# The signal between two heads' score products, from SyncE or from ScalarE

## Chip, cores and metric

One core of one Trainium2 chip runs the kernel. The metric is device time in microseconds (us) of one execution, as the median of several runs.

## What is computed

Attention with a threshold, and a two-layer network with a leaky ReLU on its result. There are 8 batches, 8 heads, 576 tokens and 64 dimensions a head; the network goes from 512 to 2048 and back to 512.

```
scores = (q @ k.T) / sqrt(64)
thresh = max(scores, axis=-1) - tau                 # tau = 0.02
scores = where(scores >= thresh, scores, -1e9)
attn   = exp(scores - max(scores))
attn   = attn / (sum(attn) + 1e-09)
x      = heads side by side of (attn @ v)           # 4608 x 512
h      = x @ w_in
out    = maximum(0.01 * h, h) @ w_out
```

## The kernel before, in words

The work is cut into 72 periods. A period takes four heads of one batch (two pairs, c = 0 and 1, of two heads, h = 0 and 1) and 128 query tokens. The last 64 tokens of each batch form periods of their own. Periods are numbered by `st.n`, and the Python loop over `n` at the end of the kernel writes out, engine by engine, what stands in each. Nothing reorders it afterwards: each engine runs its list in the order of the program, and waits are semaphores between the lists.

In period n, PE (TensorE) does in this order: the scores of period n (L297, 24 matmuls: queries and keys are split into a high and a low 16-bit half and multiplied in three combinations, `i` = 0, 1, 2); transposes of the queries or keys of later periods (L186); a transpose that spreads the reciprocal sums (L410); a piece of the network's second layer (L479); a piece of its first layer (L466); the product of weights and values of period n - 2 (L426); and again a piece of the second and of the first layer.

VectorE copies the scores out of PSUM with the row minimum of their negatives (L338), makes the thresholds (L356) and masks three of the four score tiles (L378). ScalarE has, per period: a plain exponential for each of these three tiles (L367); two leaky ReLUs of the first layer (L469); copies of transposed queries, keys and sums (L249 or L246, L416); every other period the evacuation of the second layer's bank (L488); and for the fourth tile the steep pass: a Prelu with slope 1e20 (L372) and an exponential that sums (L373), both written by `exp_steep`. This tile needs no mask from VectorE. In steady periods ScalarE's order is L249, L416, L367, L488 (every other period), L469, L367 twice, L469, L372, L373.

SP (SyncE) issues in each period a DMA transpose of the previous period's weights (L389, `turn_w`), which waits for L373 and for VectorE's masks; then loads of later queries, keys and values (L75, L99) and stores of finished rows (L496, L502). A DMA's issue occupies its queue, so what stands behind it waits.

The two heads of a pair use the upper and the lower 64 rows of PE's array and run side by side. All scores of a period lie in one PSUM tile of five banks. The bank of columns 1024 to 1535 is shared: `b12`, a piece of head 1, lies in it, and so does `a12`, a piece of head 0. [...] `scores` therefore puts b12 first among head 1's products and a12 last among head 0's, and orders a signal between them: an instruction without work (`nop`, L331) on another engine waits for the last matmul of b12, and the first weight load of a12 waits for the `nop`. The list `SIGNAL` says which engine gives it: GpSimd in periods 0, 1 and 3 to 8, SP in period 2 and from period 9 on (63 signals). On SP the `nop` of period n stands behind the loads and stores of period n - 1 and ahead of the transpose of the weights of period n - 1.

Of the kernel before, what the change touches and what calls it, by code (L numbers as in the profile page):

```python
# [33 lines left out]
def kernel(  # L34
# [10 lines left out]
    nc = tc.nc  # L45
# [182 lines left out]
    def take_high(keys, parts=1):  # L228
        for key in keys:
            for i in range(2 if key[2] == "t" else parts):  # L230
                dst, tp = place32(key, 0, i, parts)
                nc.scalar.activation(out=dst, in_=tp, func=AF.Copy, bias=0.0, scale=64.0)
# [41 lines left out]
    def pieces(c, h):  # L274
        a = PLACE[c, h]
        cut = (a // 512 + 1) * 512
        return [(a, cut - a), (cut, a + 576 - cut)]

    SIGNAL = [nc.gpsimd, nc.gpsimd, nc.sync] + [nc.gpsimd] * 6 + [nc.sync]
    HALVES = ((0, 0), (1, 0), (0, 1))  # L280

    BEHIND = mybir.DependencyInfo(mybir.DependencyClass.Sync, mybir.DependencyReason.DATA)
# [1 line left out]
    def product(st, c, h, piece, i):  # L284
        a, n = piece
        qx, kx = HALVES[i]
        rows = ds(64 * h, 64)
        key0 = 64 * (1 - h) + a - PLACE[c, h]
        for u in range(2 if st.tail else 1):
            pair = 2 * c + u if st.tail else 2 * st.pp + c  # L290
            if st.tail:
                lhs = turned[st.b, "q"][rows, qx, pair, MAIN:S]
                o = sc[ds(64 * u, 64), ds(a, n)]
            else:
                lhs = turned[st.b, "q"][rows, qx, pair, ts(st.m, 128)]
                o = sc[:, ds(a, n)]
            yield nc.tensor.matmul(out=o, lhsT=lhs, rhs=turned[st.b, "k"][rows, kx, pair, ds(key0, n)],  # L297
                                   start=(i == 0), stop=(i == 2), skip_group_check=True)
# [3 lines left out]
    def scores(st, between=None):  # L302

        st.mn = sb.tile([128, 4], FP32, tag="mn", bufs=2, name="mn")
        st.th = sb.tile([128, 4], FP32, tag="th", bufs=2, name="th")
        st.s, st.e = {}, {}
        (a00, a01), (b01, b00) = pieces(0, 0), pieces(0, 1)
        (a11, a12), (b12, b11) = pieces(1, 0), pieces(1, 1)
        todo = [[(0, a00), (0, a01), (1, a11), (1, a12)], [(1, b12), (1, b11), (0, b01), (0, b00)]]
        if st.n < 2:  # L310

            todo[1] = todo[1][2:] + todo[1][:2]
        todo = [[(c, x, i) for c, x in row for i in range(3)] for row in todo]
        at_, signal, first = [0, 0], None, None
        while todo[0] or todo[1]:
            if between and todo[0][0][0] == 1 and todo[1][0][0] == 1:
                between()
                between = None
            h = 1 if not todo[0] or (todo[1] and at_[1] < at_[0]) else 0
            if between and todo[h][0][0] == 1:  # L320
                h = 1 - h
            c, x, i = todo[h].pop(0)
            at_[h] += x[1]
            for mm in product(st, c, h, x, i):
                if first is not None:
                    tc.declare_no_dep(mm.ins, first.ins, reason="other banks")
                if (h, x) == (0, a12) and i == 0:
                    tc.add_manual_dep(mm.ins, signal.ins.name, BEHIND, reason="the row halves share a bank")
                last = mm
            if (h, x) == (1, b12) and i == 2:  # L330
                signal = SIGNAL[min(st.n, 9)].nop()  # L331
                tc.add_manual_dep(signal.ins, last.ins.name, BEHIND, reason="the row halves share a bank")
            if (h, x) == (0, a11) and i == 2 and st.n:
                first = copy_min(st, 0)

    def copy_min(st, n):
        st.s[TILES[n]] = sb.tile([128, 576], FP32, tag=f"s{n}", bufs=1, name="s")
        return nc.vector.tensor_scalar(  # L338
            out=st.s[TILES[n]][:, :], in0=sc[:, ds(PLACE[TILES[n]], 576)], scalar1=-1.0 / UNIT, scalar2=None,
            op0=AX.mult, op1=AX.min, accum_out=st.mn[:, n : n + 1])  # L340
# [19 lines left out]
    def w_of(st, t):  # L360
        c, h = t
        return st.w[:, c, :, :].rearrange("q n d -> q (n d)")[:, ds(576 * h, 576)]

    def exp_plain(st, n):
        t = TILES[n]
        st.e[t] = sb.tile([128, 576], FP16, tag=f"e{n}", bufs=1, name="e")
        nc.scalar.activation(out=st.e[t][:, :], in_=st.s[t][:, :], func=AF.Exp, bias=st.mn[:, n : n + 1], scale=-1.0)  # L367

    def exp_steep(st, n):
        c, h = t = TILES[n]  # L370
        z = st.s[t][:, :]
        nc.scalar.activation(out=z, in_=z, func=AF.Prelu, bias=st.th[:, n : n + 1], scale=-1.0, alpha=1e20)  # L372
        nc.scalar.activation(out=w_of(st, t), in_=z, func=AF.Exp, bias=minus_tau[:, :], scale=1.0,  # L373
                             accum_out=st.sum[:, c, h : h + 1])
# [77 lines left out]
    def settle():  # L452
        l2q.extend(pending)
        pending.clear()
# [18 lines left out]
    def layer2():  # L473
        g, r = l2q.pop(0)
        if r == 0:
            g.o = ps.tile([128, 512], FP32, tag="o", bufs=1, name="o")
        for j in (2 * r, 2 * r + 1):
            for c in range(2):
                nc.tensor.matmul(out=g.o[ds(64 * c, 64), :], lhsT=g.g[:, j, ds(64 * c, 64)],  # L479
                                 rhs=w_out16[:, j, :], start=(j == 0), stop=(j == 15), skip_group_check=True)  # L480
        if r == 7:
            g.out = sb.tile([128, 512], FP32, tag="osb", bufs=3, name="osb")
            if g.where == (B - 1, 3):
                a = nc.scalar.activation(out=g.out[0:64, :], in_=g.o[0:64, :], func=AF.Copy, bias=0.0, scale=1.0)
                x = nc.vector.tensor_copy(out=g.out[64:128, :], in_=g.o[64:128, :])
                tc.declare_no_dep(x.ins, a.ins, reason="other rows")
            else:
                nc.scalar.activation(out=g.out[:, :], in_=g.o[:, :], func=AF.Copy, bias=0.0, scale=1.0)  # L488
            stores.append(g)
# [141 lines left out]
    N = len(periods)  # L631
    n = 0
    while n < N + PV_LAG or l1q or pending or l2q or stores:
        st = periods[n] if n < N else None
# [8 lines left out]
        if n == 0:  # L643
            def between():
                copy_min(st, 0)
                copy_min(st, 1)
                take_low(k32[1])
                for x in now32:
                    turn32(x)
            scores(st, between)  # L650
            turn32(late)
        elif st:
            scores(st)
# [67 lines left out]
        for half in range(2):  # L721
            if half == 1 and n in (3, 4):
                exp_steep(st, plain)
            for _ in range(2):
                if l2q:
                    layer2()
            if l1q:
                layer1()
            elif n >= N:
                settle()  # L730
            if half == 0:
                if st:
                    for i in range(1, plain if n else 0):
                        exp_plain(st, i)
                        if n == 3 and i == 1:
                            take_high(late)
                if here:
                    take_w(before, 6, 6, o[:, 0:768], on_act)
                if late and n not in (0, 3):
                    turn32(late)  # L740
                    take_high(late)
                if n == N:

                    before.wt = sb.tile([128, 2, 9, 128], FP16, tag="wT", bufs=4, name="wT")
                    free = [(sc[:, ts(i, 512)].bitcast(FP16), 8 * i, m) for i, m in enumerate((8, 8, 2))]
                    for o, first, m in free:
                        turn_w_here(before, first, m, o)
                if due and n <= N:
                    if n != 3:
                        pv(due)  # L750
                    evacuate(due)
                if n == N:
                    a, *more = [take_w(before, first, m, o[:, 0 : 128 * m], on_dve if first else on_act)
                                for o, first, m in free]
                    for x in more:
                        tc.declare_no_dep(x.ins, a.ins, reason="other banks")
            elif st and n != 3:
                for i in range(plain + (n == 4), 4):
                    exp_steep(st, i)
        if n == 4:  # L760
            take_low(late)
        for i in range(plain if st else 0):
# [37 lines left out]
```

## Time and profile before

| | |
|---|---|
| median of 3 runs | 483.92 us (483.92, 486.24, 481.17) |
| the profiled execution | 484.03 us |
| its span, first to last instruction | 482.3 us |
| granted TensorE clock in it | 1.000 |
| PE busy | 463.1 us (96%) |
| VectorE (DVE) busy | 433.2 us (90%) |
| ScalarE (ACT) busy | 420.1 us (87%) |
| GpSimd (POOL) busy | 216.2 us (45%) |
| DMA transposes of weights (L389) | 68, median 6.1 us from issue to landing |

In a line of the timeline stand the start and the time that the group spans, both in us, the engine, the line of the kernel, the operation, what it writes and reads, its shape, how many there are, and in brackets how long the engine was idle before and what released it. SPq and ACTq are the instruction queues of these engines; an event semaphore there is a wait, a signal or both. PEld is PE's weight load. In a list of waits the numbers are the total in us, how often, and the longest.

### The profile page before, as it was taken

The numbers are of one execution on the slowest core, as the hardware profiler recorded it, in microseconds if no ns is written. First come the engines' busy times: TensorE is split into PE (matmuls) and PEld (weight loads), VectorE is DVE, ScalarE is ACT, GpSimd is POOL, SyncE is SP. The second block draws the span as 40 slices with busy tenths as digits, with TensorE's granted clock in tenths as the row PEclk, the third lists the DMA queues.
The fourth block names the chain that finished last, engine by engine and source line by source line (L and its number), as shares of the span: only waits on it lengthen the run. The fifth ranks groups of instructions, "written<-read, shape, count | busy, mean of one in ns | idle before, by whom it ended". The sixth has DMA issues, their size and how long they took to land.

```text
span 482.3 us, 25139 instructions
## 1 busy us (share of the span) xinstructions
PE 463.1 (96%) x10810; PEld 375.7 (78%) x10810; DVE 433.2 (90%) x1309; ACT 420.1 (87%) x783; POOL 216.2 (45%) x355
## 2 busy tenths in 40 slices
PE   6889889999999999999999999999999999999996
PEld 4668667888888888888888888788888778877774
DVE  3999879999999999999999999999999989999940
ACT  4899779999999999999999999899999889988862
POOL 2645547554565464454465474454466563000000
PEclk9999999999999999999999999999999999999999
DMA  9999999798999978899799988889889995655641
GB/s 176 237 217 197 164 206 201 160 196 182 205 171 202 209 161 188 155 173 211 154 190 202 212 174 201 135 183 193 185 183 193 200 165 124 124 122 123 127 91 46
DMA packets 206271, 83.67 MB, mean 173 GB/s; under 512 B 175280, under 2 KB 200880, under 8 KB 206160
## 3 DMA queue, kind: packets, MB, share of 16 engines
q1 hardware_dynamic: 199184, 74.66, 80.1%
q0 software_dynamic: 5568, 6.95, 7.8%
q8 instruction: 84, 1.38, 1.2%
q10 hardware_dynamic: 1408, 0.46, 0.4%
q14 instruction: 27, 0.22, 0.1%
HBM read 36.70 MB, written 9.44 MB: 96 GB/s over the span
## 4 chain that ended last, share of the span: by engine, by line
PE 86%; DMA 5%; DVE 4%; ACT 2%; issue 1%; SPq 1%; DVEq 0%; ACTq 0%
PE hp L466 25%; PE o L479 25%; PE sc L297 21%; PE pv L426 8%; DMA wT<-w 4%; PE tp L410 3%; PE tp L186 3%; DVE s L338 2%; DVE w L378 1%; DMA raw<-in_k_dram 1%; ACT g L469 1%; DVE qT L239 0%; SPq L86 0%; ACT e L367 0%; DVE kT L239 0%
## 5 line engine op out<-in xcount | busy, mean ns | idle before, releaser
L338 DVE TENSOR_SCALAR_CACHE_REDUCE s<-sc 128x576 f32<-128x576 f32 x288 | 205.5, 753 | 17.4 <-PE sc L297 17.4
L466 PEld LDWEIGHTS <-win 128*64 128x64 f16 x4608 | 146.5, 110 | 28.7 <-DVE xt L437 1.1
L378 DVE SCALAR_TENSOR_TENSOR w<-s,th,e 128x576 f16<-128x576 f32 x213 | 163.8, 817 | 0.2
L367 ACT ACTIVATE e<-s,mn 128x576 f16<-128x576 f32 x213 | 157.8, 778 | 0.0
L479 PE MATMUL o<-wout,g 128*64 128x512 f16 x1152 | 148.8, 379 | 0.3 <-DMA wout<-in_moe_w_out_dram 0.3
L466 PE MATMUL hp<-x,win 128*64 128x128 f16 x4096 | 136.3, 219 | 0.6 <-DVE x L445 0.3
L469 ACT ACTIVATE g<-hp 128x512 f16<-128x512 f32 x144 | 86.1, 598 | 43.7 <-PE hp L466 43.7
L297 PE MATMUL sc<-kT,qT 64*128 64x384 f16 (+7 forms) x1920 | 120.7, 284 | 3.5 <-DVE s L338 1.3
L297 PEld LDWEIGHTS <-qT 64*128 64x128 f16 (+1 forms) x1920 | 90.1, 97 | 20.3 <-issue 2.0
L160 POOL TENSOR_SCALAR scaled<-raw 128x512 f32<-128x512 f32 x53 | 32.7, 616 | 144.8 <-DVE w L378 131.8
L479 PEld LDWEIGHTS <-g 128*64 128x64 f16 x1152 | 58.7, 110 | 29.1 <-issue 0.4
L171 POOL TENSOR_TENSOR half<-scaled,half 128x512 f16<-128x512 f32 (+1 forms) x68 | 71.6, 1054 | 5.8
L373 ACT ACTIVATE w<-s,minus_tau 128x576 f16<-128x576 f32 x75 | 58.2, 776 | 2.4
L372 ACT ACTIVATE s<-s,th 128x576 f32<-128x576 f32 x75 | 57.5, 767 | 0.7 <-DVE th L356 0.7
L426 PE MATMUL pv<-wT,v 128*64 128x128 f16 (+1 forms) x1600 | 53.1, 215 | 5.2 <-DMA wT<-w 3.7
L426 PEld LDWEIGHTS <-v 128*64 128x64 f16 x1600 | 45.8, 110 | 6.9 <-issue 3.7
L167 POOL CAST half<-scaled 128x512 f16<-128x512 f32 (+1 forms) x68 | 38.3, 563 | 4.4
L445 DVE TENSOR_TENSOR x<-pv,by 128x256 f16<-128x256 f32 x64 | 27.1, 424 | 8.1 <-PE pv L426 7.0
L416 ACT COPY by<-tp 128x256 f16<-128x256 f16 x72 | 26.8, 372 | 0.0
L186 PEld LDWEIGHTS <-half 64*128 64x128 f16 x968 | 24.2, 95 | 2.5 <-issue 1.0
L113 POOL CAST v<-vraw 128x256 f16<-128x256 f32 x64 | 24.5, 417 | 0.0
L186 PE MATMUL tp<-ident,half 64*128 64x64 f16 x968 | 24.1, 190 | 0.0
(61 smaller groups left out, 332.9 us busy)
## 6 DMA issues: line engine op xcount, KB each, us to landing
vraw<-in_v_dram SPq DMA_DIRECT2D x16, 512.0 KB, 5.4
out_dram<-osb SPq DMA_DIRECT2D x31, 256.0 KB, 3.9
raw<-in_q_dram SPq DMA_DIRECT2D x13, 512.0 KB, 4.9
raw<-in_k_dram SPq DMA_DIRECT2D x13, 512.0 KB, 5.6
win<-in_moe_w_in_dram POOLq DMA_DIRECT2D x4, 512.0 KB, 10.7
wout<-in_moe_w_out_dram POOLq DMA_DIRECT2D x4, 512.0 KB, 12.5
raw<-in_q_dram SPq DMA_DIRECT2D x12, 128.0 KB, 3.8
raw<-in_k_dram SPq DMA_DIRECT2D x10, 128.0 KB, 4.3
```

The lines of the kernel that those rows point to most:

```text
L171: nc.gpsimd.tensor_tensor(out=halves[key][:, 1, 0:n, :, :], in0=scaled.pop(key)[:, 0:n, :, :], in1=halves[key][:, 0, 0:n, :, :], op=AX.sub ...
L186: nc.tensor.transpose(tps[key][r][:, x, t, :], half[rows, x, t, :, :].rearrange("p h d -> p (h d)"), ident[rows, rows])
L297: yield nc.tensor.matmul(out=o, lhsT=lhs, rhs=turned[st.b, "k"][rows, kx, pair, ds(key0, n)], start=(i == 0), stop=(i == 2), skip_group_ch ...
L338: return nc.vector.tensor_scalar(out=st.s[TILES[n]][:, :], in0=sc[:, ds(PLACE[TILES[n]], 576)], scalar1=-1.0 / UNIT, scalar2=None, op0=AX. ...
L367: nc.scalar.activation(out=st.e[t][:, :], in_=st.s[t][:, :], func=AF.Exp, bias=st.mn[:, n : n + 1], scale=-1.0)
L372: nc.scalar.activation(out=z, in_=z, func=AF.Prelu, bias=st.th[:, n : n + 1], scale=-1.0, alpha=1e20)
L373: nc.scalar.activation(out=w_of(st, t), in_=z, func=AF.Exp, bias=minus_tau[:, :], scale=1.0, accum_out=st.sum[:, c, h : h + 1])
L378: st.last = nc.vector.scalar_tensor_tensor(out=w_of(st, t), in0=st.s[t][:, :], scalar=st.th[:, n : n + 1], in1=st.e[t][:, :], op0=AX.is_le ...
L426: nc.tensor.matmul(out=st.pv[ds(64 * h, 64), c, ts(u, n)], lhsT=v16[st.b % 2][:, pair, blk, :], rhs=st.wt[:, c, blk - (blk > 4), ts(u, n)] ...
L466: nc.tensor.matmul(out=hp[ds(64 * c, 64), jj, :], lhsT=w_in16[:, i, ds(128 * (4 * u + jj) + 64 * c, 64)], rhs=g.x[:, i, :], start=(i == 0) ...
L469: nc.scalar.activation(out=g.g[:, ds(4 * u, 4), :], in_=hp[:, :, :], func=AF.Prelu, bias=0.0, scale=1.0, alpha=0.01)
L479: nc.tensor.matmul(out=g.o[ds(64 * c, 64), :], lhsT=g.g[:, j, ds(64 * c, 64)], rhs=w_out16[:, j, :], start=(j == 0), stop=(j == 15), skip_ ...
```

## The change

From period 9 on, ScalarE gives the signal. The steep pass of a period's fourth tile is no longer written out at the end of its own period but kept in a list, `behind_signal`, and written out in the next period's `scores`, right behind the signal. So ScalarE's queue has the signal of period n + 1 between the second L469 of period n and the steep pass (L372, L373) of period n. The earlier periods and the last one keep their order. Lines of the kernel behind the edits have numbers that are higher by 1, 3 or 7.

```diff
-    SIGNAL = [nc.gpsimd, nc.gpsimd, nc.sync] + [nc.gpsimd] * 6 + [nc.sync]
+    behind_signal = []
+    SIGNAL = [nc.gpsimd, nc.gpsimd, nc.sync] + [nc.gpsimd] * 6 + [nc.scalar]
...
             if (h, x) == (1, b12) and i == 2:
                 signal = SIGNAL[min(st.n, 9)].nop()
                 tc.add_manual_dep(signal.ins, last.ins.name, BEHIND, reason="the row halves share a bank")
+                while behind_signal:
+                    behind_signal.pop(0)()
...
             elif st and n != 3:
                 for i in range(plain + (n == 4), 4):
-                    exp_steep(st, i)
+                    if 9 <= n + 1 < N:
+
+                        behind_signal.append(lambda st=st, i=i: exp_steep(st, i))
+                    else:
+                        exp_steep(st, i)
```

In the built program PE's, VectorE's and GpSimd's lists are the same as before but for the semaphore that PE's 63 weight loads wait for. ScalarE's list has 63 event semaphores more, SP's has 63 fewer.

## The prediction

> **What bounds the kernel now.** I read the page's busy times first, then the chain that ended last, then PE's timeline of one steady period, then the waits by engine, and last the timelines of SP and ScalarE beside PE's. Busy time and chain agree that PE sets the end:
>
> ```profile
> PE 463.1 (96%) x10810; PEld 375.7 (78%) x10810; DVE 433.2 (90%) x1309; ACT 420.1 (87%) x783; POOL 216.2 (45%) x355
> PE 86%; DMA 5%; DVE 4%; ACT 2%; issue 1%; SPq 1%; DVEq 0%; ACTq 0%
> ```
>
> So a change counts only by how much it moves PE. One steady period on PE:
>
> ```profile
> 251.58 1.64 PE L297 MATMUL sc<-kT,qT 64*128 64x384 f16 x24
> 253.06 0.40 PE L186 MATMUL tp<-ident,half 64*128 64x64 f16 x16
> 253.39 0.30 PE L410 MATMUL tp<-ident,rec 128*64 128x128 f16 x4
> 253.52 1.03 PE L479 MATMUL o<-wout,g 128*64 128x512 f16 x8
> 254.39 1.06 PE L466 MATMUL hp<-x,win 128*64 128x128 f16 x32
> 255.28 0.73 PE L426 MATMUL pv<-wT,v 128*64 128x128 f16 x20
> 255.84 1.03 PE L479 MATMUL o<-wout,g 128*64 128x512 f16 x8
> ```
>
> The next scores start at 257.69, so a period is 6.11 us and its 24 score products run without a gap. Here the signal is not on the path. In the trace its event on SP stands at 252.116, 0.54 us after the scores start; the weight load that needs it starts at 252.579, 0.08 us behind the load before it, which is PE's pace. A signal reaches a waiting load in 0.04 us (the smallest distance seen), so 0.4 us is spare.
>
> The waits from 360 to 400 us, and then PE and SP there, show where it is late:
>
> ```profile
> PEld L297 <- SPq L331: 1.8, 2, 1.1
> PE sc L297 <- SPq L331: 1.1, 2, 0.8
> ```
>
> ```profile
> 382.64 0.50 PE L297 MATMUL sc<-kT,qT 64*128 64x256 f16 x5 [0.34 <-SPq L331]
> ...
> 387.61 1.32 PE L297 MATMUL sc<-kT,qT 64*128 64x384 f16 x19
> 389.74 0.50 PE L297 MATMUL sc<-kT,qT 64*128 64x256 f16 x5 [0.81 <-SPq L331]
> ```
>
> ```profile
> 383.28 5.25 SPq L389 DMA_TRANSPOSE wT<-w  x1
> 388.58 1.04 SPq L502 DMA_DIRECT2D out_dram<-osb  x2
> ```
>
> SP issued a transpose for 5.25 us and then two stores, so its signal, next in the queue, came at 389.67 where 388.15 would have been in step. The products that it stands for, the first three of the second head, had ended at 388.11. Of the 63 signals from period 9 on, three made PE wait: at 277.08, 382.64 and 389.73.
>
> ScalarE around the place where the signal is to go:
>
> ```profile
> 251.69 0.60 ACT L469 ACTIVATE g<-hp 128x512 f16<-128x512 f32 x1 [0.39 <-PE hp L466]
> 252.18 0.77 ACT L372 ACTIVATE s<-s,th 128x576 f32<-128x576 f32 x1
> 252.98 0.77 ACT L373 ACTIVATE w<-s,minus_tau 128x576 f16<-128x576 f32 x1
> ...
> 253.76 0.56 ACT L249 COPY kT<-tp 128x512 f16<-128x512 f16 x1
> 254.22 0.37 ACT L416 COPY by<-tp 128x256 f16<-128x256 f16 x1
> 254.48 0.78 ACT L367 ACTIVATE e<-s,mn 128x576 f16<-128x576 f32 x1
> 255.16 0.59 ACT L488 ACTIVATE osb<-o 128x512 f32<-128x512 f32 x1
> ```
>
> ScalarE waits for PE ahead of L469, then runs without a pause to L488, the evacuation of the output bank, which PE needs for its second layer at 255.84.
>
> **Removed: 63 signals on SP.** The gain is what PE lost to late ones. Score starts 380.98, 387.61 and 394.70 make periods of 6.63 and 7.09 us against 6.11: 0.52 + 0.98 = 1.50 us. The late one at 277.08 costs nothing: its period is 6.13. In all other periods the cover is SP being early. SP also saves an event and its successor's 0.08 us in each period, worth nothing: the transpose behind it waits for the steep pass of L373 anyway and starts 0.12 us after it ends in 67 of 68 cases. Loads and stores stay in their order. Bounds for the gain: 0 if PE then waits elsewhere for the same queue, and about 3 us if this execution is a mild one (the three runs span 481.17 to 486.24).
>
> Would PE wait elsewhere? The transpose of 383.28 landed at 390.51, and PE needs it for the pv product at 392.29, which would come at 392.29 - 0.66 - 1.12 = 390.51 (the two late loads, 0.74 and 1.20 us behind their neighbours, less 0.08 each). That is just in time. I keep 1.50.
>
> **Added: 63 signals on ScalarE, each with a wait for PE.** Queued behind it are L372, L373, then the copies, L367 and L488; SP's transpose waits for L373, PE for the copies, DVE for e, PE for L488. First the signal: L469 itself waits for the layer product just ahead of the scores and starts 0.11 us after they do, so the event can go at the same 0.54 us at which SP's goes now, in every period, with 0.4 us to spare. No PE time is lost on it.
>
> Now the delay of L372. Today its own event, which checks VectorE, stands at 251.697, 0.006 us after L469 starts, and L372 starts at 252.184, 0.10 us before L469 ends. In the new order the signal goes 0.427 us after the start of L469; the next event follows a signal by 0.078 us on SP's and GpSimd's queues; on ScalarE an instruction starts 0.056 us after its event when the engine is free (L249 at 191.99). That gives 0.561 us against 0.493 today: a delay of 0.07 us. The trace has no signal on ScalarE, so I bound it: 0.00 if event and dispatch hide in L469's run, and 0.24 if the signal goes only when L469 has ended (0.597 + 0.078 + 0.056 - 0.493). I take 0.07, because both rows it is built from are of this mechanism.
>
> [...] The trace shows an overlap of 0.10.
>
> Who feels 0.07 us? For each PE instruction that waits for ScalarE I took its start less the end of the releaser. Layer one after L469 has 0.46 us or more in nine of ten cases, pv after L416 0.62, VectorE's masks after e 0.37; these cover it. The output bank after L488 has not: 0.05 us is the handing over itself, and most of the 33 cases after 80 us stand at 0.05 to 0.09. Taking 0.068 less the spare of each (and less ScalarE's pauses ahead of L488) leaves 17 cases and 0.58 us. At 0.24 it would be 4.5 us, at 0.00 nothing. In the periods without L488 ScalarE's 0.22 us pause ahead of L469 takes it up.
>
> SP's transposes start 0.07 us later too. Five periods are already 0.12 to 0.21 us long because pv waits for a landing (pv at 175.00 is one); 5 x 0.07 = 0.34 us. At 0.24 it is 1.2.
>
> **The steep pass that is recorded later** now stands behind VectorE's masks and ahead of the next period's copies in the program's text. Each engine's own list is the same but for the signals: PE, VectorE and GpSimd unchanged, ScalarE +63 events, SP -63. Cost nothing; the only waits with other numbers are PE's on the signal.
>
> **Sum.** The profiled execution took 484.03 us (span 482.3): 484.03 - 1.50 + 0.58 + 0.34 = 483.45. It stands 0.11 above the median of 483.92. Predicted: 483.4 us, within 1% of before, which is about what a measurement of this kernel can tell from no change.
>
> **Rivals.**
> *Slower: the signal waits for L469's end.* Place: ScalarE, each period. Price: delay 0.24, so 4.5 us at the output bank and 1.2 at landings, less 1.50: 484.03 + 4.2 = 488.2. It decides once the delay passes 0.11 us, where banks (1.2) and landings (0.5) eat the gain. Against it: the event of L372 goes 0.006 us after L469 starts, not after its end. [...]
> *Faster: late signals are what makes the runs differ.* If the median of runs loses 3 us of them, 484.03 - 3.0 + 0.9 = 481.9. For it: 5 us between three runs, and SP's transposes take 2.5 to 7.2 us to issue. Against it: only three of 63 signals were late here, in an execution at the median.
> *Nothing gained: the transfer is the wait.* PE reaches pv earlier and stands there for the transpose: 484.03 + 0.9 = 484.9. For it: the zero margin at 390.51.
> *The signal comes no earlier.* Only if ScalarE itself were late; its pause ahead of L469 is 0.22 us or more in every period from 10 on. Practically out.
>
> **How the numbers follow.** Forecast 0.50; landing wait 0.20; late signals 0.17; L469's end 0.13. The forecast alone spans 482.5 to 484.2, its delay going from 0.00 to 0.10 us (at 0.10: banks 1.13, landings 0.50). The range goes to 481.0 on the side of the late signals and to 486.4 on the other, about half way to 488.2. Faster than 479.1 takes more late signals than any run here shows room for: 0.04. Slower than 488.8 takes the delay of 0.24 with no gain: 0.06. Within: 0.90.
>
> **What would show it.** Right: no wait of L297 for a signal; the two periods near 385 back at 6.1 us; L372 starting 0.56 us after L469 rather than 0.49; PE's second-layer start after L488 at 0.05 us throughout. Wrong: L372 at 0.7 us or more; pv waiting for wT by as much as the signal did; or periods that are longer everywhere by over 0.1 us.

## The result and the profile after

| | before | after |
|---|---|---|
| median of 22 runs each, us | 482.34 | 484.33 |
| lowest and highest, us | 480.18 and 486.24 | 481.39 and 488.42 |
| the profiled execution, us (its span) | 484.03 (482.3) | 484.98 (483.2) |
| granted TensorE clock in it | 1.000 | 0.996 |

The ratio is 1.0044, with a 95% interval of [1.0023, 1.0064]: slower by about 2 us. One run of the change, at 490.26 us, is left out of its highest time and of the ratio because it lies over 1.5% above the fastest. The time lies within 1% of before and within the predicted range, but on the other side of no change than the forecast. The first three runs of before had a median of 483.92 us, and the forecast's sum started from one of 484.03; over 22 runs the median is 482.34.

Lines behind the edits have higher numbers now: L466 and L469 (layer one and its leaky ReLU) are L469 and L472, L372 and L373 (the steep pass) are L375 and L376, L479 and L488 (layer two and its evacuation) are L482 and L491, L426 (pv) is L429, L331 (the signal) is L332.

Busy times and shares of the chain of the changed kernel:

```profile
PE 465.6 (96%) x10810; PEld 379.3 (78%) x10810; DVE 432.6 (90%) x1309; ACT 424.6 (88%) x783; POOL 216.1 (45%) x355
PE 83%; DMA 6%; ACT 5%; DVE 4%; issue 2%; SPq 0%; DVEq 0%
```

PE bounds it as before. ScalarE's share of the chain went from 2% to 5%, and that of SP's queue from 1% to 0. Its waits from 72 to 415 us (total, how often, longest):

```profile
ACT s L375 <- ACT g L472: 1.5, 6, 0.3
...
PE pv L429 <- DMA wT<-w: 0.6, 2, 0.3
PE o L482 <- ACT osb L491: 0.5, 3, 0.2
```

No wait for the signal is in that list: the lines `PEld L297 <- SPq L331` are gone, and nothing like them has come on ScalarE's queue. The three rows shown are among those that before's list doesn't have. ScalarE and PE in the steady period that the prediction showed:

```profile
253.06 0.60 ACT L472 ACTIVATE g<-hp 128x512 f16<-128x512 f32 x1 [0.39 <-PE hp L469]
253.63 0.78 ACT L375 ACTIVATE s<-s,th 128x576 f32<-128x576 f32 x1
254.44 0.78 ACT L376 ACTIVATE w<-s,minus_tau 128x576 f16<-128x576 f32 x1
...
255.94 0.78 ACT L370 ACTIVATE e<-s,mn 128x576 f16<-128x576 f32 x1
256.62 0.59 ACT L491 ACTIVATE osb<-o 128x512 f32<-128x512 f32 x1
```

```profile
252.94 1.65 PE L298 MATMUL sc<-kT,qT 64*128 64x384 f16 x24
256.64 0.72 PE L429 MATMUL pv<-wT,v 128*64 128x128 f16 x20
257.26 1.05 PE L482 MATMUL o<-wout,g 128*64 128x512 f16 x8
258.12 1.09 PE L469 MATMUL hp<-x,win 128*64 128x128 f16 x32
259.14 1.07 PE L298 MATMUL sc<-kT,qT 64*128 64x384 f16 x15
```

In before, the groups behind the second layer's start at 255.84 were:

```profile
256.70 1.06 PE L466 MATMUL hp<-x,win 128*64 128x128 f16 x32
257.69 1.65 PE L297 MATMUL sc<-kT,qT 64*128 64x384 f16 x24
```

L375 starts 0.57 us after L472 where it was 0.49. The delay runs on through ScalarE to L491, whose end PE awaits: L482 starts 0.62 us after pv where it was 0.56, it and the group behind it take 1.05 and 1.09 where they took 1.03 and 1.06, and the period is 6.20 where it was 6.11.

ScalarE at 104 us, and PE's second layer behind it, show what the forecast had not at all:

```profile
104.36 0.60 ACT L472 ACTIVATE g<-hp 128x512 f16<-128x512 f32 x1 [0.47 <-PE hp L469]
105.21 0.77 ACT L375 ACTIVATE s<-s,th 128x576 f32<-128x576 f32 x1 [0.26 <-ACT g L472]
```

```profile
108.84 1.05 PE L482 MATMUL o<-wout,g 128*64 128x512 f16 x8 [0.17 <-ACT osb L491]
```

Here ScalarE stood idle for 0.26 us with all waits met: the last event ahead of L375 ends at 104.885, L375 starts at 105.210. It happens in periods 14, 23, 32, 41, 50 and 59, the six cases of the list above. I call it a pause. In 14, 32 and 50 an evacuation of the bank follows, and these three periods take 6.47 us.

Where the two late signals had been, PE now stands a little later, for the transposed weights:

```profile
393.32 0.75 PE L429 MATMUL pv<-wT,v 128*64 128x128 f16 x20 [0.28 <-DMA wT<-w]
```

**Where the time went.** From the start of period 10 to that of period 64 before took 334.2, 334.2 and 334.4 us in its three profiled executions, the change 334.9 and 336.6 in its two. For each of these periods I took its length less the shortest that it has in any run of this study whose order of work is like the change's or before's. That excess falls into three parts. "Banks" are all excesses below 0.1 us, "pauses" periods 14, 32 and 50 above that, the rest is irregular (late signals, landings). In us:

| | banks | pauses | irregular | sum |
|---|---|---|---|---|
| before, three profiled executions | 0.26, 0.33, 0.44 | 0 | 2.67, 2.57, 2.69 | 2.99 in the mean |
| the change, two | 1.47, 1.40 | 1.08, 1.08 | 1.17, 2.92 | 4.56 in the mean |

Banks and pauses cost 2.2 us more (the three paused periods hold 3 x 0.084 of bank wait, too). The irregular part is smaller by 0.6 here, and by 0.86 over all nine executions of this study with the signal on ScalarE at its normal place (1.79 against 2.64 in the mean). The net of these parts, 1.3 to 1.6 us, compares with 1.7 to 2.1 us by the ratios of the repeated runs (1.0036 in e9 and 1.0044 here); the rest is within what single executions scatter.

### The profile page after: what moved, and what is told of

Its sections match the earlier page's. It is cut to its first block, busy times and chain, and to the rows that moved or that the text cites. A ratio compares the mean times of both kernels' runs of the same rounds, so it can differ in the third digit from the quotient of the medians.

```text
span 483.2 us, 25140 instructions
## 1 busy us (share of the span) xinstructions
PE 465.6 (96%) x10810; PEld 379.3 (78%) x10810; DVE 432.6 (90%) x1309; ACT 424.6 (88%) x783; POOL 216.1 (45%) x355
## 4 chain that ended last, share of the span: by engine, by line
PE 83%; DMA 6%; ACT 5%; DVE 4%; issue 2%; SPq 0%; DVEq 0%
PE hp L469 24%; PE o L482 24%; PE sc L298 20%; PE pv L429 8%; DMA wT<-w 5%; PE tp L413 3%; PE tp L186 3%; DVE s L341 2%; ACT g L472 1%; DMA raw<-in_k_dram 1%; ACT s L375 1%; DVE w L381 1%; ACT w L376 1%; ACT e L370 1%; ACT kT L249 1%
## 5 line engine op out<-in xcount | busy, mean ns | idle before, releaser
L469 PEld LDWEIGHTS <-win 128*64 128x64 f16 x4608 | 147.9, 110 | 28.4 <-issue 1.3
L482 PE MATMUL o<-wout,g 128*64 128x512 f16 x1152 | 149.5, 380 | 0.5 <-ACT osb L491 0.5
L469 PE MATMUL hp<-x,win 128*64 128x128 f16 x4096 | 137.4, 220 | 0.6 <-DVE x L448 0.3
L472 ACT ACTIVATE g<-hp 128x512 f16<-128x512 f32 x144 | 86.1, 598 | 39.4 <-PE hp L469 37.2
L482 PEld LDWEIGHTS <-g 128*64 128x64 f16 x1152 | 60.4, 110 | 29.2 <-issue 1.2
L376 ACT ACTIVATE w<-s,minus_tau 128x576 f16<-128x576 f32 x75 | 58.2, 776 | 2.4
L375 ACT ACTIVATE s<-s,th 128x576 f32<-128x576 f32 x75 | 58.2, 776 | 2.4 <-ACT g L472 1.5
L429 PE MATMUL pv<-wT,v 128*64 128x128 f16 (+1 forms) x1600 | 53.1, 215 | 4.5 <-DMA wT<-w 3.0
L429 PEld LDWEIGHTS <-v 128*64 128x64 f16 x1600 | 45.8, 110 | 5.7 <-DMA wT<-w 2.7
```

The source lines that it names most:

```text
L429: nc.tensor.matmul(out=st.pv[ds(64 * h, 64), c, ts(u, n)], lhsT=v16[st.b % 2][:, pair, blk, :], rhs=st.wt[:, c, blk - (blk > 4), ts(u, n)] ...
L469: nc.tensor.matmul(out=hp[ds(64 * c, 64), jj, :], lhsT=w_in16[:, i, ds(128 * (4 * u + jj) + 64 * c, 64)], rhs=g.x[:, i, :], start=(i == 0) ...
L472: nc.scalar.activation(out=g.g[:, ds(4 * u, 4), :], in_=hp[:, :, :], func=AF.Prelu, bias=0.0, scale=1.0, alpha=0.01)
```

## The experiments

Two theories were put to the test. A: the loss is made on ScalarE, because an instruction that waits for PE stands in its queue, and it is felt at the output bank. B: it comes from SP, whose transposes now start elsewhere, and from their landings. Within A two readings of the pauses stood open: A1, they are bound to a count of ScalarE's instructions (they come 128 apart if events and reads of the accumulator are counted); A2, they are bound to the place behind the signal.

**e1_between: the signal between the two halves of the steep pass.** The Prelu is written out at once, only the summing exponential stands behind the signal.

```diff
-    def exp_steep(st, n):
+    def exp_steep(st, n, later=False):
...
+        if later:
+            behind_signal.append(lambda: exp_sum(st, n))
+        else:
+            exp_sum(st, n)
...
-                        behind_signal.append(lambda st=st, i=i: exp_steep(st, i))
+                    exp_steep(st, i, later=9 <= n + 1 < N)
```

> The signal stays on ScalarE, but stands between the two halves of the steep pass: the Prelu ahead of it, the summing exponential behind. Theory A (the signal holds ScalarE's queue, so the Prelu starts late and the output bank is evacuated late): the Prelu starts 0.49 us after the leaky ReLU as before, not 0.57; the 0.84 us starts are gone; second-layer waits for the output bank fall back to the handing over; no wait of PE for a signal; ratio to before 0.997 to 1.001. Theory B (the time comes from SP: with its signals gone, transposes and loads go at other moments, and PE waits for landings): this changes nothing on SP against the changed kernel, so ratio 1.003 to 1.006.

Measured 481.66 us, ratio to before 0.9982 [0.9953, 1.0011]. Its ScalarE and PE:

```profile
251.01 0.60 ACT L480 ACTIVATE g<-hp 128x512 f16<-128x512 f32 x1 [0.39 <-PE hp L477]
251.51 0.77 ACT L375 ACTIVATE s<-s,th 128x576 f32<-128x576 f32 x1
252.31 0.78 ACT L384 ACTIVATE w<-s,minus_tau 128x576 f16<-128x576 f32 x1
...
254.49 0.59 ACT L499 ACTIVATE osb<-o 128x512 f32<-128x512 f32 x1
```

```profile
255.16 1.03 PE L490 MATMUL o<-wout,g 128*64 128x512 f16 x8
256.02 1.06 PE L477 MATMUL hp<-x,win 128*64 128x128 f16 x32
257.02 1.64 PE L298 MATMUL sc<-kT,qT 64*128 64x384 f16 x24
```

The Prelu is back at 0.49 us, layer two at 1.03, the period at 6.11, no pause can be seen, and no signal is late: the event goes at 251.442, behind the Prelu in the queue. The engine that signals is the same as in the change, and SP's list too, so the place in ScalarE's queue makes the loss. Where it is felt, e1 alone leaves open: SP's transposes, too, start again 2.29 us after the scores as in before (median), where they start at 2.38 in the change. e3 tells the two apart.

**e2_phase: four tiny activations more at the start,** so that every later instruction of ScalarE has a number higher by four.

```diff
-    nc.scalar.activation(out=waste[:, :], in_=minus_tau[:, :], func=AF.Exp, bias=0.0, scale=1.0)
+    for _ in range(5):
+        nc.scalar.activation(out=waste[:, :], in_=minus_tau[:, :], func=AF.Exp, bias=0.0, scale=1.0)
```

> The changed kernel with four tiny activations more at the start, where ScalarE waits for the first loads; they shift the place in ScalarE's instruction count by 4. Theory A1 (a pause of 0.27 us at every 128th instruction of ScalarE, which the changed kernel's 128 instructions per nine periods pin to the Prelu behind the signal): the six Prelu starts at 0.85 us after the leaky ReLU are gone, all at 0.57 to 0.60; the three periods of 6.47 us are 6.20; ratio 1.002 to 1.003. Theory A2 (the pause belongs to what these periods do): the six stay where they are, ratio 1.004.

Measured 484.47 us, ratio 1.0048 [1.0028, 1.0068]. The six starts at 0.85 us are gone and periods 14, 32 and 50 take 6.20: A1 holds, A2 doesn't. A ratio of 1.002 to 1.003 had been expected; the time did not fall. Its profile has one long wait for a landing that the change's has not:

```profile
PE pv L429 <- DMA wT<-w: 1.5, 1, 1.5
```

**e3_bank_first: the evacuation of the output bank ahead of the first plain exponential,** everything else as in the change.

```diff
-            exp_plain(st, 0)
+            if n < 9:
+                exp_plain(st, 0)
...
+            if half == 0 and st and n >= 9:
+                exp_plain(st, 0)
```

> The changed kernel, but from period 9 on ScalarE evacuates the output bank ahead of the first plain exponential of the period. Theory A: the 0.08 us at the Prelu and the 0.27 us pauses stay, but PE's second-layer start no longer waits (spare of 0.5 us or more in place of 0.05); steady periods at 6.11; ratio 0.998 to 1.001. Theory B: the bank was not the place, ratio 1.003 to 1.006. If VectorE's masks now wait for the exponential, periods grow, ratio over 1.004.

Measured 482.81 us, ratio 1.0009 [0.9979, 1.0039]. ScalarE and PE near the end of the evacuation:

```profile
252.43 0.60 ACT L491 ACTIVATE osb<-o 128x512 f32<-128x512 f32 x1
252.93 0.77 ACT L370 ACTIVATE e<-s,mn 128x576 f16<-128x576 f32 x1
...
255.64 0.60 ACT L472 ACTIVATE g<-hp 128x512 f16<-128x512 f32 x1
256.21 0.78 ACT L375 ACTIVATE s<-s,th 128x576 f32<-128x576 f32 x1
```

```profile
253.68 1.03 PE L482 MATMUL o<-wout,g 128*64 128x512 f16 x8
254.54 1.06 PE L469 MATMUL hp<-x,win 128*64 128x128 f16 x32
```

The Prelu is as late as in the change (0.57) and pauses six times, but L491 ends 0.65 us before PE needs it (median; below 0.06 in none of 33 cases), and layer two takes 1.03 again. The bank excess falls to 0.17 us, and the steady periods with a bank take 6.11 again. SP's transposes start as late as in the change (2.38 us after the scores). So the output bank is where the delay is felt, and B is out as the main cause. The trace carries this, not the time, whose interval overlaps that of the change.

**e4_later: the signal waits for two products more,** to see what a larger delay costs.

```diff
-            if (h, x) == (1, b12) and i == 2:
+            if (h, x, i) == ((1, b11, 0) if st.n >= 9 else (1, b12, 2)):
```

> The changed kernel, but its signal waits for the first product of the next piece of the same head, two products later. Theory A: the Prelu starts some 0.15 us later again (0.70 to 0.75 us after the leaky ReLU); about 17 to 22 output-bank waits grow by that, 2.5 to 3.5 us in all; ratio 1.008 to 1.012. The signal itself still has 0.2 us to spare. Theory B: no change against the changed kernel, ratio 1.003 to 1.006.

Measured 488.73 us, ratio 1.0133 [1.009, 1.0175].

```profile
254.19 0.60 ACT L472 ACTIVATE g<-hp 128x512 f16<-128x512 f32 x1 [0.39 <-PE hp L469]
254.92 0.78 ACT L375 ACTIVATE s<-s,th 128x576 f32<-128x576 f32 x1
```

The Prelu starts at 0.74 us (median), 26 of 33 banks make PE wait, and the steady ones of their periods take 6.36: 0.25 for a delay of 0.25. It cost more than forecast, 6 us, and one for one with the delay in these periods.

**e5_both: e1 and e3 together.**

> Both remedies at once: the signal between Prelu and summing exponential, and the output bank evacuated ahead of the first plain exponential. Theory A: no wait for a signal, none for the bank; steady periods all 6.11 us, so also the 0.04 us that five bank waits cost before are gone; ratio to before 0.995 to 1.000. If the landings of the transposes are what is left, PE's waits for wT stay and vary from run to run by 1 to 2 us.

Measured 481.56 us, ratio 0.9988 [0.996, 1.0016]. No bank makes PE wait (0.65 us spare), but two periods are long for landings (6.64 and 7.19). Against e1 nothing is gained that can be measured.

**e6_behind: only the engine of the signal changes;** the steep pass stays at the end of its period and so ahead of the signal.

```diff
-    SIGNAL = [nc.gpsimd, nc.gpsimd, nc.sync] + [nc.gpsimd] * 6 + [nc.sync]
+    SIGNAL = [nc.gpsimd, nc.gpsimd, nc.sync] + [nc.gpsimd] * 6 + [nc.scalar]
```

> ScalarE gives the signal, but its steep pass stands ahead of it in the queue, so only the order of the two is undone. If a signal goes as soon as the instruction ahead has left ScalarE's wait (the exponential waits for the Prelu's end, 1.29 us after the leaky ReLU starts), it comes 1.4 us after the scores start where 0.96 is needed: PE waits 0.45 us in each of 63 periods, 28 us in all, ratio 1.05 to 1.07. If it goes only when the instruction ahead has ended, 0.8 us more: 75 to 85 us, ratio 1.15 to 1.18. If ScalarE's place in the queue did not matter: ratio 1.00.

Measured 499.58 us in two runs, ratio 1.0347 [1.0286, 1.0408]. Its waits and ScalarE (line numbers as before):

```profile
PEld L297 <- ACTq L331: 24.0, 52, 0.5
...
PE sc L297 <- ACTq L331: 7.3, 46, 0.2
```

```profile
252.81 0.77 ACT L372 ACTIVATE s<-s,th 128x576 f32<-128x576 f32 x1
253.60 0.78 ACT L373 ACTIVATE w<-s,minus_tau 128x576 f16<-128x576 f32 x1
```

The signal goes at 253.611, 0.007 us after L373 starts and 0.77 before it ends: here the event did not wait for the end of what stood ahead of it. The order in the queue is worth 17 us. Less was lost than expected, since a late weight load cost PE 0.14 us less than it waited: 0.48 us of wait made each period 0.33 longer (6.45 against 6.11).

**e7_before_again and e8_before_again: the kernel before, profiled twice more.**

> The kernel before, profiled once more, to see whether late signals belong to it. If the 1.5 us of PE waits for the signal are a part of this kernel, two or three of its 63 signals on SP are late again, near 277, 383 and 390 us. If they were chance of the one execution, they are absent or elsewhere, and the gain that the change could have is smaller than 1.5 us.

> As the run ahead of it: a third look at the kernel before, for how many signals on SP are late and what they cost in sum; 1.5 us again if they are a part of the kernel, 0 to 1 us if they are chance.

Measured 482.96 and 483.84 us, one run each. The late signals recur, with 1.22 and 2.35 us of load waits in the two. The second's, from 72 to 415 us:

```profile
PEld L297 <- SPq L331: 2.3, 3, 1.2
PE sc L297 <- SPq L331: 1.3, 2, 0.9
```

Their periods are longer by 0.69 and 1.87 us, by 1.50 in the first execution: 1.35 in the mean. They are a part of the kernel and no accident of one run.

**e9_change_again and e10_between_again: the change and e1 on the same chip.**

> The changed kernel once more, beside the next run on the same chip: ratio to before 1.002 to 1.006. In its profile the six late Prelu starts of 0.85 us stand at the same instructions and 16 to 18 output-bank waits are there; both come from ScalarE's order alone and do not vary. PE's waits for landings do vary and stand where the late signals of before stood, near periods 42 and 60, if SP's queue and the transfers are what these signals were late for.

> The signal between Prelu and summing exponential, once more. Theory A gives 2.2 us less than the changed kernel on the same chip (1.4 of bank waits, 0.8 of pauses): ratio to before 0.996 to 1.001, and 0.994 to 0.997 against the changed kernel. Whether it beats before depends on how much of the late signals' time comes back as waits for landings: all of it and the ratio is 1.000, none and it is 0.996.

The change 484.31 us, 1.0036 [1.0014, 1.0058], with the same six pauses and the same banks. Its waits for landings were expected near periods 42 and 60; the long ones came in 43 and 57. e1's kernel 482.38 us, 0.9978 [0.9953, 1.0003], so 1.9 us below the change by the medians. It beats the change; against before its two intervals both still touch 1. From period 10 to 64 its two executions took 332.5 and 333.2 us, below all three of before.

**e11_phase_again and e12_phase_one: four tiny activations at the start once more, and one.** The diff is e2's, with `range(2)` in e12.

> The changed kernel with four more tiny activations on ScalarE at the start, a second time, because the first profile showed the six pauses gone from the Prelu and yet the time was not lower. If the pauses are part of the loss: the Prelu starts at 0.57 us after L472 in periods 14 to 59, periods 14, 32 and 50 take 6.20 us, and the ratio to before is 1.0020 to 1.0030, about 0.8 us below the changed kernel's 1.0036 to 1.0044. If what the pauses cost is given back at landings of the transposed weights, or is not felt: the profile is the same but the ratio stays at 1.0036 to 1.0048.

> The changed kernel with one more tiny activation on ScalarE at the start, so that each 128th instruction is the second L472 of a period rather than the Prelu behind the signal. L472 is preceded by 0.2 to 0.4 us in which ScalarE waits for TensorE. If the pause is bound to the count of instructions: no Prelu of periods 14 to 59 at 0.85 us after L472, and L472 starts at the usual distance behind the layer product or up to 0.27 us later in six periods. If the pauses are part of the loss, the ratio to before is 1.0020 to 1.0030; if they are not felt, or given back at landings, 1.0036 to 1.0048.

e11 482.75 us, 1.0012 [0.999, 1.0034]; e12 483.94 us, 1.0038 [1.0007, 1.0068]. In e11 the pauses are gone again. In e12 they are not, against what I expected:

```profile
104.61 0.60 ACT L472 ACTIVATE g<-hp 128x512 f16<-128x512 f32 x1 [0.47 <-PE hp L469]
105.48 0.78 ACT L375 ACTIVATE s<-s,th 128x576 f32<-128x576 f32 x1 [0.27 <-ACT g L472]
```

But they have moved by exactly one instruction. In the change the time passes between the last event ahead of L375 (104.868) and L375 (105.210), 0.34 us for 0.06 elsewhere. In e12 it passes between the signal (105.042) and that event (105.415), 0.37 us for 0.08, and L375 follows the event by 0.06. I had left the events out when I reckoned that one step leads to L472; the number counts them. So A1 is shown to the instruction. What the pauses cost in the repeated runs isn't: on one chip the kernel without them was 1.2 us faster at the median (in the mean 1.6, interval about [0.1, 3.1]), but e2, the same kernel as e11, had shown nothing. Its 1.0048 and e11's 1.0012 also say that a ratio repeats less well than one interval tells.

## Why the prediction was right and wrong

**The step that failed: "added", what the delay costs.** The prediction set 0.58 us at the output bank and 0.34 at landings against a gain of 1.50, and so forecast 0.6 us less. The runs show 1.3 to 1.4 us at the bank and a further 0.8 that no term held, against a gain of about 0.9. That the forecast of 483.4 stands only 0.9 us from the measured 484.33 is partly luck: its starting point was 1.7 us above the median of before.

**Right: the signal is never late on ScalarE.** It goes 0.54 to 0.57 us after the scores start in all of periods 10 to 63 (predicted 0.54), the weight load follows it by 0.44 us or more without waiting, and the two periods near 385 lost their waits for it.

**Right: the rival of L469's end is out.** e6 shows the event 0.007 us behind the start of the instruction ahead of it, and 0.77 us before that one's end.

**Right but small: the delay.** Predicted 0.07 us, measured 0.084 (0.493 to 0.577); event to event is 0.080 where 0.078 was taken, event to start 0.062 for 0.056. L375 now starts 0.02 us before L472 ends, where the overlap had been 0.10.

**In the step "added", the place was right and the size wrong.** The output bank feels the delay (e3), but the term of 0.58 us measures 1.3 to 1.4 (banks 1.44 - 0.34, and 3 x 0.084 in the paused periods). The spare of the 33 cases was known to a few hundredths, and the term hangs on them: 0.016 us more of delay adds that in each of some 17 cases, and a wait of 0.06 us cost PE 0.084, since layer one behind it also took 0.02 longer to the next scores (1.02 us from start to start, in e1 1.00).

**What no step held: ScalarE's pause,** 0.27 to 0.29 us, six times, 128 instructions apart, three of them ahead of a bank: 3 x 0.27 = 0.8 us. In before the event of L372 stood 0.006 us after L469's start, and 0.487 us before L372's, so the queue was half a microsecond ahead of the engine. e6, with the order of before, shows that such a lead hid the pause: in the same six periods the event of L373, which has the numbers 192 to 832 in the order of the queue, follows that of L372 by 0.37 to 0.38 us instead of 0.087, and the Prelu starts at 0.494 us all the same. The signal, which waits for PE, takes this lead away: in the change 0.062 us lie between the event and the start of L375. Nine periods hold 119 instructions of ScalarE in before and 128 in the change, so in the change the pause comes back to the same instruction every nine periods, and it is the one behind the signal.

**The step "removed": the 1.50 us.** The amount is there in three executions (1.35 in the mean), but only about 0.9 comes back, a figure good to some 0.5, since landings scatter. The prediction saw the zero margin of the transpose at 390.51 and kept the 1.50 all the same. In the changed kernel PE waits for a landing there (0.28 us at 393.32, behind the latest of the signals, and 0.30 at 281.58). That was the rival "the transfer is the wait", and by these means it holds for about a third of the sum.

**Landings, 0.34,** can't be told from the scatter of landings between executions (irregular 0.88 to 2.92 us with the signal on ScalarE).

So the sum with the measured terms is 484.03 - 0.9 + 1.4 + 0.8 = 485.3 against 484.98 of the profiled execution. That they come so close is in part chance: from period 10 to 64 these two executions differ by only 0.7 us, because few landings were late in the change's; another 0.4 arose ahead of period 10, and 0.2 was saved behind 64.

The rival "late signals make the runs differ" fell: they are gone, and the runs still spread by 7.0 us. The traces show a larger source: period 10 starts between 76.1 and 80.0 us in the 14 profiled executions, while the stretch from period 64 to the end takes 69.0 to 69.2 us in all but e6.

**Open:** what the pauses cost in the repeated runs; what makes them, which no run here shows; and why some landings come late.

## What to carry to other kernels

A wait put into an engine's queue can cost more than its own time: here it also took the lead that the queue had on the engine (0.487 us in before, 0.062 in the change), and with it the cover of small delays behind it. Put it where the engine still has a long instruction in hand, here between Prelu and exponential rather than ahead of both: the same signal, 1.9 us less. And a late wait on the critical engine is worth only what stands behind it: look for the next releaser before booking it as a gain (here about 0.9 of 1.50 us came back).

## What was not expected of the hardware

- In the change ScalarE paused for 0.27 to 0.29 us at six instructions of its stream that lie 128 apart, events and accumulator reads counted (numbers 192, 320, 448, 576, 704 and 832). In e12, with one instruction more ahead of them, the pause stood one instruction earlier (0.37 us from the signal to the event behind it, 0.08 elsewhere). In the change it delayed the Prelu (0.85 us after L472 starts, 0.577 in the median); in e6 the events show it (0.37 to 0.38 us for 0.087) and the Prelu does not (0.494 us after the leaky ReLU).
- In the change, the event behind the signal in ScalarE's queue went 0.080 us after it, and the free engine started 0.062 us after its event.
- A late weight load cost PE 0.14 us less than it waited (0.48 of wait, 0.33 of time in e6; 0.66 and 0.52 in before), and a wait of a matmul for a bank cost a little more (0.06 and 0.084 in the change).
